# Two-batch score streaming, flat K transposes and a later norm and softmax in a decode-attention kernel

## The chip, the cores and the metric

The kernel runs on one core of one Trainium2 chip. The metric is device microseconds of one execution, and lower is better. Each run has a time, and a profile of one execution whose span is about 2 us shorter than its time. Some executions of a program are slower than the fastest of the same kernel by over 1.5%; they are called slow, and comparisons here use the others ("fast"). The *granted clock* is the share of full speed at which the profile shows TensorE running.

## The reference

Two independent problems, A and B, each a decode step of grouped-query attention with a window, are computed and joined at the end:

```python
# x (2,1,576)  wq (576,4096)  k_cache, v_cache (2,16,16384,128)  wo (4096,576), all bf16
q = (x @ wq).reshape(B, 1, 32, 128)              # 32 query heads, 16 key/value heads
k = repeat(k_cache[:, :, Sk-4096:], 2, axis=1)   # the last 4096 positions
v = repeat(v_cache[:, :, Sk-4096:], 2, axis=1)
p = softmax(einsum("bhqd,bhkd->bhqk", q, k) * 128**-0.5)
out = einsum("bhqk,bhkd->bhqd", p, v).reshape(B, 1, 4096) @ wo
# ... the same for B, then concatenated along the last axis
```

Each key/value head needs 2 MB of K and 2 MB of V (both batches), used once. With wq and wo the kernel reads 153.1 MB.

## The kernel before

A *slab* is one key/value head of one problem, both batches together: 32 slabs in all. Four slabs make a *group*, and the softmax runs once per group. Partitions hold (row, batch) pairs, so the kernel turns each K slab round before its score matmuls. VectorE does that with block transposes of fp32 words (each two bf16 values; 3592 ns for 128 x 2048 words in the profile of before). The kernel's patterns take a row in blocks of 32 words that hold both batches mixed, and the old transpose sorts the batches apart while it writes:

```python
# X: half a K slab, 128 x 2048 fp32 words; the write jumps between the batches' halves of a block
Xop[(t, jb)] = S.add("dve", lambda e: e.transpose(
    xt[:, n % NXT, :].bitcast(FP32).rearrange("p (c b r) -> p c r b", b=Bb, r=16),
    ring[:, r, jb * HW_:(jb + 1) * HW_].bitcast(FP32).rearrange("p (c r b) -> p c r b", b=Bb, r=16)), deps, ...)
# S: scores, one batch at a time, 8 matmuls of 512 columns for a half slab
for b in range(Bb):
    for p4 in range(4):
        o = 64 * b32 + 32 * b + par
        mv = bass.AP(b0.tensor, b0.offset, [list(b0.ap[0]), [128, 32], [2, 16]])
        last = e.matmul(st[:, 0:512], zq[:, p4, m, b, 16 - 16 * jb:144 - 16 * jb], mv, ...)
```

After the exps, P is transposed (pT), and four masked multiplications build pC, which has zeros where a V row belongs to the other batch. PV multiplies 64 tiles of V by 56 columns of pC. The *norm* divides by the softmax's sum. Instructions of an engine run in the order in which this loop adds them (in the slab shown further down, the transpose at 196.65 us starts only after the norm, for which VectorE had waited 3.75 us):

```python
for t in range(NSLAB + LAG):                 # LAG = 4
    i = t - LAG
    if t < NSLAB:
        for jb in range(2):
            make_X(t, jb)                    # VectorE
            make_S(t, jb)                    # TensorE
        # ... make_Z
        if t % 4 == 3:
            make_chain(t // 4)               # max, bias, exp, pT, pC, sum: all engines
    if i >= 0:
        make_PV(i)                           # TensorE
        make_norm(i)                         # VectorE: waits for PV(i)
        # ... projection
```

K and V slabs pass through a ring of eight slots. One queue issues the loads (q1 of the page, 153.10 MB), in the order of the program. A slot is loaded anew when its last reader (the second transpose for K, PV for V) is done. The *lag* is the number of slabs by which PV follows the K transposes in the loop.

Of the kernel before, what the change touches and what calls it, by code (L numbers as in the profile page):

```python
# [59 lines left out]
def build_kernel(nc, probs, out):  # L60
# [3 lines left out]
    LAG = 4  # L64
# [12 lines left out]
    SCALE = float(Dh) ** -0.5  # L77

# [14 lines left out]
    with es:  # L93
# [5 lines left out]
        zq = sb("zq", [128, 4, 4, 2, 144], BF16)  # L99
# [3 lines left out]
        qs = sb("qs", [128, NPROB, 4, Hq * Bb], BF16)  # L103
# [6 lines left out]
        pmask = sb("pmask", [128, 2], FP32)  # L110
        bmask = sb("bmask", [128, 4], FP32)
        hmask = sb("hmask", [128, 8], FP32)
        m1 = sb("m1", [128, 1], FP32)
        nM = sb("nM", [1, 16], FP32)
        nMrep = sb("nMrep", [1, 128], FP32)
        bias_sb = sb("bias_sb", [128, 1], FP32)
# [5 lines left out]
        pT = sb("pT", [128, 2, 512], BF16)  # L122
        PCW = 1024
        pC = sb("pC", [128, 2, PCW + 64], BF16)
# [6 lines left out]
        ST = [ps("st%d" % i) for i in range(2)]  # L131
        OT = [ps("ot%d" % i) for i in range(2)]
        PJ = [ps("pj%d" % i) for i in range(2)]
# [61 lines left out]
        p_zq = S.add("pool", lambda e: e.memset(zq[:].rearrange("d p m b w -> d (p m b w)").bitcast(FP32), 0.0), [], "zero_zq")  # L195
        p_zpc = S.add("pool", lambda e: e.memset(pC[:, :, PCW:PCW + 64], 0.0), [], "zero_pC")

        d_xs0 = S.add("dve", lambda e: e.memset(xtf[0:Bb, 0:NPROB * 4 * D].bitcast(FP32), 0.0), [], "zero_xs")

        def f_xs(e):  # L200
            last = None
            for h in range(2):
# [4 lines left out]
        d_pm = S.add("dve", lambda e: e.tensor_reduce(pmask[:, 0:2], ident_f[:].rearrange("p (i t) -> p t i", t=2), AX.X, ALU.add),  # L207
                     [p_ident_f], "pmask")
# [37 lines left out]
        for P in range(NPROB):  # L246
# [22 lines left out]
            def f_qs(e, bank, P=P):  # L269
# [6 lines left out]
                qs[:, P, :, :], bank[:, 0:256].rearrange("d (p w) -> d p w", p=4), ACTF.Copy), [op], "qsev%d" % P)  # L276
# [25 lines left out]

        def contiguous_wo(G):
            return G < NG - 1

# [51 lines left out]
        pC_op = {}  # L357
# [6 lines left out]
        def make_Z(t):  # L364
            P, g = t // Hkv, t % Hkv
            m = t % 4
            deps = [qs_ev[P], p_zq, d_bm]
            if t >= 4:
                deps.append(Sop[(t - 4, 1)])

            def f(e):
                last = None
                for p4 in range(4):
                    b0 = zq[:, p4, m, 0, 16 + 4 * m:16 + 4 * m + 1]
                    dst = bass.AP(b0.tensor, b0.offset, [list(b0.ap[0]), [32, 4], [144 + 2, Bb], [1, 2]])
                    src = qs[:, P, p4, 4 * g:4 * g + 4].rearrange("d (h b) -> d b h", b=Bb).unsqueeze(1).broadcast_to([128, 4, Bb, 2])
                    msk = bmask[:, 0:4].unsqueeze(2).unsqueeze(3).broadcast_to([128, 4, Bb, 2])
                    last = e.tensor_tensor(dst, src, msk, ALU.mult)  # L378
                return last
            Zop[t] = S.add("pool", f, deps, "Z%d" % t)  # L380

        def make_X(t, jb):
# [7 lines left out]
            else:  # L390
                deps.append(op_xT)
            Xop[(t, jb)] = S.add("dve", lambda e: e.transpose(  # L392
                xt[:, n % NXT, :].bitcast(FP32).rearrange("p (c b r) -> p c r b", b=Bb, r=16),
                ring[:, r, jb * HW_:(jb + 1) * HW_].bitcast(FP32).rearrange("p (c r b) -> p c r b", b=Bb, r=16)),
                deps, "X%d_%d" % (t, jb))
# [3 lines left out]
        def make_S(t, jb):  # L399
            G, m = t // 4, t % 4  # L400
            n = 2 * t + jb
            st = ST[G % 2]
            deps = [Xop[(t, jb)], Zop[t]]
            if m == 0 and jb == 0 and G >= 2:
                deps.append(exp_op[G - 2])

            def f(e):
                last = None
                for b in range(Bb):
                    for p4 in range(4):  # L410
                        b32, par = p4 // 2, p4 % 2
                        o = 64 * b32 + 32 * b + par
                        b0 = xt[:, n % NXT, o:o + 1]
                        mv = bass.AP(b0.tensor, b0.offset, [list(b0.ap[0]), [128, 32], [2, 16]])
                        first = m == 0 and jb == 0 and b == 0 and p4 == 0
                        last = e.matmul(st[:, 0:512], zq[:, p4, m, b, 16 - 16 * jb:144 - 16 * jb], mv,  # L416
                                        start=first, stop=True, skip_group_check=True)
                return last
            Sop[(t, jb)] = S.add("pe", f, deps, "S%d_%d" % (t, jb))

        APH = dict(a=8, p=8, h=2)

        def make_chain(G):
# [3 lines left out]
            mx = S.add("dve", lambda e: e.tensor_reduce(m1[:], st[:, :], AX.X, ALU.max), [Sop[(4 * G + 3, 1)]] + prev("Tm"), "max%d" % G)  # L427
            n1, b1, tm = tb_job(lambda e, bank: e.transpose(bank[0:1, 0:128], m1[:, 0:1], ident_f[:]), "Tm%d" % G, [mx, p_ident_f])  # L428
            chain[(G, "Tm")] = tm
            nm = S.add("dve", lambda e: e.tensor_reduce(nM[0:1, 0:16].rearrange("o (p h) -> o p h", p=8),  # L430
                                                        b1[0:1, 0:128].rearrange("o (a p h) -> o p h a", **APH),
                                                        AX.X, ALU.max, negate=True), [tm] + prev("nMrep"), "nM%d" % G)
            tb_consumer[n1] = nm
            chain[(G, "nMrep")] = S.add("dve", lambda e: e.tensor_scalar(  # L434
                nMrep[0:1, :].rearrange("o (a c) -> o a c", a=8), nM[0:1, 0:16].unsqueeze(1).broadcast_to([1, 8, 16]),
                SCALE, None, ALU.mult), [nm] + prev("bias"), "nMrep%d" % G)
            n2, b2, bi = tb_job(lambda e, bank: e.matmul(bank[:, 0:1], nMrep[0:1, 0:128], ones_f[0:1, 0:1], start=True, stop=True),  # L437
                                "bias%d" % G, [chain[(G, "nMrep")], p_ones_f])
            chain[(G, "bias")] = bi
            bc = S.add("act", lambda e: e.activation(bias_sb[:, 0:1], b2[:, 0:1], ACTF.Copy),  # L440
# [3 lines left out]
            for w in range(2):  # L444
                def f_exp(e, w=w):
                    if w == 0:
                        dst = pR[:, 0, :].rearrange("p (q r x) -> p q x r", r=16, x=2)
                    else:
                        b0 = pR[:, 1, 1:2]
                        dst = bass.AP(b0.tensor, b0.offset, [list(b0.ap[0]), [32, 16], [-1, 2], [2, 16]])  # L450
                    return e.activation(dst, st[:, :].rearrange("p (q x r) -> p q x r", x=2, r=16), ACTF.Exp,  # L451
                                        bias=bias_sb[:, 0:1], scale=SCALE, **({"accum_out": rsum[:, 0:1]} if w == 0 else {}))
                exs.append(S.add("act", f_exp, [bc] + prev("Ts") + prev("pT%d" % w), "exp%d_%d" % (G, w)))
            exp_op[G] = exs[1]
            n3, b3, ts = tb_job(lambda e, bank: e.transpose(bank[0:1, 0:128], rsum[:, 0:1], ident_f[:]), "Ts%d" % G, [exs[0], p_ident_f])  # L455
            chain[(G, "Ts")] = ts
            pts = []
            for w in range(2):
                chain[(G, "pT%d" % w)] = S.add("dve", lambda e, w=w: e.transpose(pT[:, w, :], pR[:, w, :]),  # L459
                                               [exs[w]] + prev("pC"), "pT%d_%d" % (G, w))  # L460
                pts.append(chain[(G, "pT%d" % w)])
            deps = pts + [d_pm, p_zpc]
            if G >= 2:
                deps.append(PVop[4 * (G - 2) + 3])

            def f_pc(e):
                last = None
                for b in range(Bb):
                    for w in range(2):
                        jp = b ^ w  # L470
                        src = pT[:, w, :].rearrange("k (q s b h) -> k s q b h", q=16, s=8, b=Bb)[:, :, :, b, :]
                        dst = pC[:, v, 0:PCW].rearrange("k (s q j b h) -> k s q j b h", s=8, q=16, j=2, b=Bb)[:, :, :, jp, b, :]
                        last = e.tensor_scalar(dst, src, pmask[:, b:b + 1], None, ALU.mult)  # L473
                return last
            chain[(G, "pC")] = S.add("dve", f_pc, deps, "pC%d" % G)
            pC_op[G] = chain[(G, "pC")]
            sm = S.add("dve", lambda e: e.tensor_reduce(ssum[0:1, 0:16].rearrange("o (p h) -> o p h", p=8),
                                                        b3[0:1, 0:128].rearrange("o (a p h) -> o p h a", **APH),
                                                        AX.X, ALU.add), [ts] + prev("rs"), "ssum%d" % G)
            tb_consumer[n3] = sm  # L480
            chain[(G, "rs")] = S.add("dve", lambda e: e.reciprocal(rs[0:1, 0:16], ssum[0:1, 0:16]), [sm] + prev("rsbm"), "rs%d" % G)  # L481
            n4, b4, rb = tb_job(lambda e, bank: e.matmul(bank[:, 0:16], ones_f[0:1, 0:128], rs[0:1, 0:16], start=True, stop=True),  # L482
# [8 lines left out]
        def make_PV(i):  # L491
# [9 lines left out]
            for j0, j1, dma in parts:  # L501
                def f(e, j0=j0, j1=j1):
                    last = None
                    for j in range(j0, j1):
                        jb, q, jp = j // 32, (j % 32) // 2, j % 2
                        col = ((jb * 4 + m) * 16 + q) * 8 + jp * 4
                        last = e.matmul(ot[:, 0:NS], ring[:, r, j * 128:(j + 1) * 128], pC[:, v, col:col + NS],  # L507
                                        start=(j == 0), stop=(j == KR - 1))
# [196 lines left out]
```

## Time and profile before

| | before |
|---|---|
| time, median (its range) | 468.87 us (467.79 to 469.25) |
| span of the profiled execution (which took 467.26 us) | 465.5 us |
| queue of the loads, share of 16 engines | 79.6% |
| VectorE / TensorE busy | 58% / 62% |
| mean granted TensorE clock | 0.795 |

These are lines of the kernel before's page: the TensorE clock, the DMA share (tenths) and the rate in 40 slices of the span, the queue of the loads, the chain of waits that ended last, and three groups of instructions (busy time, mean ns of one, idle time of the engine before them and what ended it).

```profile
PEclk9958977787687877886796785878868777788779
DMA  8999999999999946999379974499848994897000
GB/s 355 435 412 428 428 427 427 422 430 429 416 370 429 401 183 265 427 429 418 127 306 429 377 315 182 176 424 405 352 190 327 429 423 188 336 394 275 1 0 4
...
q1 hardware_dynamic: 11700, 153.10, 79.6%
...
DVE 49%; PE 40%; DMA 6%; issue 3%; ACT 1%; SPq 0%
...
L392 DVE STREAM_TRANSPOSE xt<-ring 128x2048 f32<-128x2048 f32 x64 | 225.0, 3592 | 21.2 <-DMA ring<-in_A_k_cache_dram 21.2
L416 PE MATMUL st<-xt,zq 128*128 128x512 bf16 x512 | 166.3, 483 | 108.2 <-DVE xt L392 107.6
...
L522 DVE TENSOR_TENSOR oTg<-ot,rsb 128x4 bf16<-128x4 f32 x32 | 5.2, 162 | 123.0 <-PE ot L507 123.0
```

The rate row starts at a plateau of about 427 GB/s and later has holes (183, 127, 176). At 427 GB/s the 153.1 MB would take 359 us. So the loads could be 100 us faster than the kernel, and the chain holds VectorE and TensorE, not DMA. No engine is full, because they take turns. The norm itself is 5.2 us of work, but VectorE stands idle for 123 us in front of it.

One ordinary slab, from the timeline of the kernel before (start us, duration us, engine, line, operation, and in brackets the idle time before and what ended it):

```profile
185.78 7.05 DVE L392 STREAM_TRANSPOSE xt<-ring 128x2048 f32<-128x2048 f32 x2
...
189.42 5.46 PE L416 MATMUL st<-xt,zq 128*128 128x512 bf16 x16 [3.76 <-DVE xt L392]
...
194.72 1.81 PE L507 MATMUL ot<-pC,ring 128*128 128x56 bf16 x64
...
196.57 0.16 DVE L522 TENSOR_TENSOR oTg<-ot,rsb 128x4 bf16<-128x4 f32 x1 [3.75 <-PE ot L507]
196.65 3.59 DVE L392 STREAM_TRANSPOSE xt<-ring 128x2048 f32<-128x2048 f32 x1
```

VectorE transposes for 7.05 us, then waits 3.75 us until TensorE has done the second half's scores and PV, does a norm of 0.16 us, and only then begins the next slab: 10.87 us from transpose to transpose (196.65 - 185.78). Once per group a softmax stands between as well, with no K transpose beside it: from the maximum at 217.7 us to the first PV at 224.4.

### The profile page before, as it was taken

Reading aid. Unit: us, or ns where it says so; the run is one execution under the profiler, and the core shown is the slowest. Engines: PE = TensorE matmul, PEld = TensorE weight load, DVE = VectorE, ACT = ScalarE, POOL = GpSimd, SP = SyncE. Lnnn points to the kernel's source line nnn. Section 1 sums busy time; section 2 is a strip of 40 time slices with the busy share of each in tenths; the row PEclk is TensorE's granted clock in tenths of the full one; section 3 lists DMA queues with packets and bytes.
Section 4 is the critical chain, followed back from the end, with each engine's and each line's share of the span. In section 5 each row is a group of like instructions: output and inputs, shape, how many; then the busy total and the mean of one; then the engine's idle time right before and its main releaser. Section 6 shows DMA issues by size and latency. Waiting matters only on the chain.

```text
span 465.5 us, 6840 instructions
## 1 busy us (share of the span) xinstructions
PE 287.1 (62%) x3124; PEld 156.4 (34%) x3124; DVE 269.3 (58%) x206; ACT 19.4 (4%) x50; POOL 30.2 (6%) x144
## 2 busy tenths in 40 slices
PE   1556535665866658656555656575586665865667
PEld 1552112331533334222433314232153323422155
DVE  3029966566666636665664662656666663666530
ACT  1000010001000010001000010000100001000010
POOL 5100100000000000000000000000000000000000
PEclk9958977787687877886796785878868777788779
DMA  8999999999999946999379974499848994897000
GB/s 355 435 412 428 428 427 427 422 430 429 416 370 429 401 183 265 427 429 418 127 306 429 377 315 182 176 424 405 352 190 327 429 423 188 336 394 275 1 0 4
DMA packets 11741, 153.54 MB, mean 330 GB/s; under 512 B 1208, under 2 KB 2240, under 8 KB 2368
## 3 DMA queue, kind: packets, MB, share of 16 engines
q1 hardware_dynamic: 11700, 153.10, 79.6%
q8 instruction: 24, 0.39, 0.3%
q14 instruction: 5, 0.04, 0.0%
q10 hardware_dynamic: 12, 0.01, 0.0%
HBM read 153.10 MB, written 0.00 MB: 329 GB/s over the span
## 4 chain that ended last, share of the span: by engine, by line
DVE 49%; PE 40%; DMA 6%; issue 3%; ACT 1%; SPq 0%
DVE xt L392 40%; PE st L416 22%; PE ot L507 14%; DMA ring<-in_A_k_cache_dram 6%; DVE pT L459 2%; DVE pC L473 2%; PE pj L571 1%; DVE m L427 1%; DVE oTg L522 1%; PE tb L482 1%; ACT pR L451 1%; PE tb L437 1%; PE tb L551 1%; PE pj L539 1%; DVE nM L430 0%
## 5 line engine op out<-in xcount | busy, mean ns | idle before, releaser
L392 DVE STREAM_TRANSPOSE xt<-ring 128x2048 f32<-128x2048 f32 x64 | 225.0, 3592 | 21.2 <-DMA ring<-in_A_k_cache_dram 21.2
L416 PE MATMUL st<-xt,zq 128*128 128x512 bf16 x512 | 166.3, 483 | 108.2 <-DVE xt L392 107.6
L416 PEld LDWEIGHTS st<-xt,zq 128*128 128x128 bf16 x512 | 53.0, 114 | 212.1 <-DVE xt L392 138.0
L522 DVE TENSOR_TENSOR oTg<-ot,rsb 128x4 bf16<-128x4 f32 x32 | 5.2, 162 | 123.0 <-PE ot L507 123.0
L507 PEld LDWEIGHTS ot<-pC,ring 128*128 128x128 bf16 x2048 | 66.2, 102 | 6.7 <-issue 1.6
L507 PE MATMUL ot<-pC,ring 128*128 128x56 bf16 x2048 | 68.0, 196 | 0.0
L378 POOL TENSOR_TENSOR zq<-qs,bmask 128x16 bf16<-128x16 bf16 x128 | 23.5, 216 | 355.6 <-PE st L416 341.7
L571 PE MATMUL pj<-wob,oP 128*2 128x288 bf16 x112 | 24.1, 396 | 4.9 <-DVE oP L563 4.9
L459 DVE STREAM_TRANSPOSE pT<-pR 128x512 bf16<-128x512 bf16 x16 | 11.4, 712 | 12.6 <-ACT pR L451 12.6
L482 PE MATMUL tb<-rs,ones_f 1*128 1x16 f32 x16 | 4.8, 379 | 21.5 <-DVE rs L481 21.5
L254 PE MATMUL tb<-xU,ring 128*128 128x56 bf16 x288 | 12.5, 219 | 8.0 <-DMA ring<-in_B_wq_dram 5.8
L571 PEld LDWEIGHTS pj<-wob,oP 128*2 128x2 bf16 x112 | 11.8, 110 | 14.6 <-DVE oP L563 5.6
L427 DVE TENSOR_REDUCE m<-st 128x1 f32<-128x512 f32 x8 | 5.5, 691 | 19.3 <-PE st L416 19.3
L440 ACT ACTIVATE bias_sb<-tb 128x1 f32<-128x1 f32 x8 | 1.4, 171 | 364.1 <-PE tb L437 364.1
L254 PEld LDWEIGHTS tb<-xU,ring 128*128 128x128 bf16 x288 | 12.3, 119 | 8.2 <-DMA ring<-in_B_wq_dram 5.9
L451 ACT ACTIVATE pR<-st,bias_sb 128x512 bf16<-128x512 f32 x16 | 12.7, 818 | 0.3
L482 PEld LDWEIGHTS tb<-rs,ones_f 1*128 1x128 f32 x16 | 4.0, 305 | 23.3 <-DVE rs L481 23.3
L473 DVE TENSOR_SCALAR pC<-pT,pmask 128x256 bf16<-128x256 bf16 x32 | 8.4, 335 | 0.3
L236 PE MATMUL tb<-ident_b,xt 2*128 2x2 bf16 x36 | 2.3, 194 | 9.8 <-DVE xt L204 9.8
L455 PE MATMUL tb<-ident_f,rsum 128*1 128x128 f32 x8 | 2.5, 308 | 9.3 <-ACT pR L451 9.3
L437 PE MATMUL tb<-ones_f,nMrep 1*128 1x1 f32 x16 | 3.0, 256 | 4.9 <-DVE nMrep L434 4.9
L428 PE MATMUL tb<-ident_f,m 128*1 128x128 f32 x8 | 2.2, 270 | 6.3 <-DVE m L427 6.3
(42 smaller groups left out, 46.3 us busy)
## 6 DMA issues: line engine op xcount, KB each, us to landing
ring<-in_A_k_cache_dram SPq DMA_DIRECT2D x16, 2048.0 KB, 20.7
ring<-in_A_v_cache_dram SPq DMA_DIRECT2D x16, 2048.0 KB, 12.7
ring<-in_B_k_cache_dram SPq DMA_DIRECT2D x16, 2048.0 KB, 9.4
ring<-in_B_v_cache_dram SPq DMA_DIRECT2D x15, 2048.0 KB, 9.9
ring<-in_A_wq_dram SPq DMA_DIRECT2D x1, 4608.0 KB, 13.5
ring<-in_B_wq_dram SPq DMA_DIRECT2D x1, 4608.0 KB, 25.4
wob<-in_A_wo_dram SPq DMA_DIRECT2D x4, 1152.0 KB, 15.5
wob<-in_B_wo_dram SPq DMA_DIRECT2D x4, 1152.0 KB, 10.4
```

What stands on the lines that cost most here:

```text
L254: last = e.matmul(bank[:, c * 64:c * 64 + NS], wqv[P][:, u, cb * 128:(cb + 1) * 128], xU[:, P, u, 0:NS], start=(u == 0), stop=(u == NU - 1))
L378: last = e.tensor_tensor(dst, src, msk, ALU.mult)
L392: Xop[(t, jb)] = S.add("dve", lambda e: e.transpose(xt[:, n % NXT, :].bitcast(FP32).rearrange("p (c b r) -> p c r b", b=Bb, r=16), ring[:, ...
L416: last = e.matmul(st[:, 0:512], zq[:, p4, m, b, 16 - 16 * jb:144 - 16 * jb], mv, start=first, stop=True, skip_group_check=True)
L427: mx = S.add("dve", lambda e: e.tensor_reduce(m1[:], st[:, :], AX.X, ALU.max), [Sop[(4 * G + 3, 1)]] + prev("Tm"), "max%d" % G)
L451: return e.activation(dst, st[:, :].rearrange("p (q x r) -> p q x r", x=2, r=16), ACTF.Exp, bias=bias_sb[:, 0:1], scale=SCALE, **({"accum_ ...
L459: chain[(G, "pT%d" % w)] = S.add("dve", lambda e, w=w: e.transpose(pT[:, w, :], pR[:, w, :]), [exs[w]] + prev("pC"), "pT%d_%d" % (G, w))
L473: last = e.tensor_scalar(dst, src, pmask[:, b:b + 1], None, ALU.mult)
L482: n4, b4, rb = tb_job(lambda e, bank: e.matmul(bank[:, 0:16], ones_f[0:1, 0:128], rs[0:1, 0:16], start=True, stop=True), "rsbm%d" % G, [ch ...
L507: last = e.matmul(ot[:, 0:NS], ring[:, r, j * 128:(j + 1) * 128], pC[:, v, col:col + NS], start=(j == 0), stop=(j == KR - 1))
L522: norm_op[i] = S.add("dve", lambda e: e.tensor_tensor(oTg[:, v, 2 * m:2 * m + 2, :], OT[i % 2][:, 0:4].rearrange("d (b h) -> d h b", h=2), ...
L571: last = e.matmul(PJ[half][0:Bb, 0:NH], oP[:, v, j, :], wob[:, v, j, half * NH:(half + 1) * NH], start=(proj_start(G) and j == 0), stop=Tr ...
```

## The change

The intent has four parts. (a) The K transpose writes flat. (b) The *masked path*: score matmuls stream both batches' columns as they lie, into two banks per group; columns of the foreign batch get a bias of -1e30 in the exp and so become zeros, and transposed P feeds PV directly, without pC and its multiplications (so here the bias is the mask; "the old masked pC path" below means before's). (c) The norm comes after the next slab's first transpose, and the softmax is spread over the next group's first slab. (d) The lag goes from 4 to 5. The core of the diff, with cuts:

```diff
-    LAG = 4
+    LAG = 5
+    OFF = -1.0e30
...
             Xop[(t, jb)] = S.add("dve", lambda e: e.transpose(
-                xt[:, n % NXT, :].bitcast(FP32).rearrange("p (c b r) -> p c r b", b=Bb, r=16),
-                ring[:, r, jb * HW_:(jb + 1) * HW_].bitcast(FP32).rearrange("p (c r b) -> p c r b", b=Bb, r=16)),
-                deps, "X%d_%d" % (t, jb))
+                xt[:, n % NXT, :].bitcast(FP32), ring[:, r, jb * HW_:(jb + 1) * HW_].bitcast(FP32)), deps, "X%d_%d" % (t, jb))
...
-                for b in range(Bb):
+                for jl in range(2):
                     for p4 in range(4):
-                        o = 64 * b32 + 32 * b + par
+                        o = 2048 * jl + 64 * b32 + par
-                        mv = bass.AP(b0.tensor, b0.offset, [list(b0.ap[0]), [128, 32], [2, 16]])
+                        mv = bass.AP(b0.tensor, b0.offset, [list(b0.ap[0]), [128, 16], [2, 32]])
...
+            for jb in range(2):
+                def f_exp(e, jb=jb):
+                    for t in range(2):          # columns of batch t: foreign rows have the bias OFF
+                        last = e.activation(pR[:, jb, :].rearrange("p (x t) -> p t x", t=2)[:, t, :],
+                                            st[jb][:, :].rearrange("p (x t) -> p t x", t=2)[:, t, :], ACTF.Exp,
+                                            bias=bias_sb[:, t:t + 1], scale=SCALE, accum_out=...)
...
-                        last = e.matmul(ot[:, 0:NS], ring[:, r, j * 128:(j + 1) * 128], pC[:, v, col:col + NS],
+                        last = e.matmul(ot[:, 0:NS], ring[:, r, j * 128:(j + 1) * 128], pT[:, v, col:col + NS],
...
-        for t in range(NSLAB + LAG):
+        for t in range(NSLAB + LAG + 1):
             i = t - LAG
+            # X(t,0) S(t,0) | max, bias, exp of group t//4-1 when t%4 == 0 | norm(i-1) |
+            # X(t,1) S(t,1) | pT, sum of that group | PV(i) | projection
```

## The prediction

> **What bounds it now.** Not the transfers. The page's 40 slices show about 427 GB/s at first, then holes (183, 127, 176); 153.1 MB at 427 would take 359 us, the span is 465.5. The queue's own waits: 208 us for the K transpose, 133 for PV; consumers free the eight slots too late. The chain of waits alternates VectorE's K transposes (40%), scores (22%) and PV (14%). In the timeline an ordinary slab is two transposes of 3.52 us, scores (1.90 us, 3.4 at half clock), PV 1.67-1.81, and a norm of 0.16 that in-order VectorE awaits 3.7-5.9 us before the next transpose: 10.8-12.6 us. Once per four slabs the softmax (217.7 to 227.5 us) runs with no K transpose beside it. A group takes about 54 us; its transfers need 4 x 9.8 + 2.8 = 42.
>
> **What changes.**
> 1. Order. Norm and softmax move half a slab or more later: under the next transpose TensorE does scores and PV, under the second exp runs. With the old transpose time, an ordinary slab becomes scores 2.6 + PV 2.1 (means over both clocks) + 0.3 + 3.5 = 8.5 us; a group's first about 16 (the transposes of max and sum queue behind scores), its second 10.7: 44 us a group.
> 2. Flat K transpose. It writes consecutive fp32 words, not words 64 bytes apart. The 512-element pT takes 712 ns; [...]2048 would be about 2.3 us, not 3.59. [...]If so, 64 x 1.25 = 80 us of VectorE go, and a group needs 37 us. Chance 70%.
> 3. pC goes: 32 x 335 ns, 1 us a group.
> 4. Added: a second maximum per group (+0.7 us), doubled small max and bias work (1 us), four half-size exps with four accumulator reads for two (+0.7 us, hidden). TensorE's work is unchanged: 512 score matmuls of 512 columns, 2048 of PV. Strided PSUM reads may cost a little.
> 5. Lag 5 for 4: one more slab at the end, hidden behind V loads.
>
> **How much is on the path.** Nearly all of 1-3, until transfers bind. With the fast transpose a group (37 us) is under its loads (42): bound by transfers. The first 116 us move 48.8 MB at 419 GB/s, the other 104.3 MB at 428 take 244: last byte near 361 us. Then short PV, norm, projection, copy, output: 4 us as at before's end; 1.8 from span to device time. About 368. With the old transpose: first scores near 32, 44 a group, a tail of 20: about 392. Weighted: **371 us, 8 in 10 from 364 to 396**. Faster by over 2%: 0.98; within 2%: 0.01; slower: 0.01.
>
> **What would show it.** DMA at 9 in every slice until the end; the queue's waits for consumers down; the transpose's waits for K loads up; mean transpose 2.3 us (3.5 is the miss); no pC lines; norm's wait for PV (123 us) below 40; VectorE busy about 190 us; mean clock about 0.8.
>
> **What would make it wrong.** The transpose stays at 3.5 us (390 or more); stride-2 PSUM reads double maxima and exps; score matmuls read xt or write PSUM slower; half clock for most of the time, so that scores plus PV take 10 us a slab; group-boundary waits that hold the ring; wo loads, held in order behind a projection, that open holes.

The 2.3 us stands as a forecast only ("If so" refers to it). The sum: 64 x 1.25 = 80 us of VectorE, 37 us a group, branches of 368 and 392 us, and 371 put between them.

## The result, and the profile after

| | before | after |
|---|---|---|
| time, median (range), 4 runs each | 468.87 (467.79 to 469.25) | 371.17 us (370.97 to 372.71) |
| span | 465.5 | 369.0 us |
| queue of the loads | 79.6% | 98.0% |
| VectorE busy | 269.3 | 185.9 us |
| mean granted clock | 0.795 | 0.857 |

The ratio is 0.793, 95% interval 0.790 to 0.795. A ratio here is always the mean time of one kernel's fast runs over that of the other's in the same rounds, so not quite the ratio of the medians. The lines of the changed kernel's page that answer to those of before:

```profile
PEclk9978999898589888998588888999578886996898
DMA  8999999999999999999999999999999999999992
GB/s 320 448 414 426 426 425 433 428 426 426 429 424 424 426 423 435 424 428 426 423 431 424 426 426 427 430 425 428 420 430 428 427 423 426 428 424 420 424 418 121
...
q1 hardware_dynamic: 11700, 153.10, 98.0%
...
DMA 87%; DVE 10%; PE 2%; SPq 1%; issue 0%
...
L392 DVE STREAM_TRANSPOSE xt<-ring 128x2048 f32<-128x2048 f32 x64 | 146.0, 2292 | 100.7 <-DMA ring<-in_A_k_cache_dram 56.5
L413 PE MATMUL st_0<-xt,zq 128*128 128x512 bf16 x256 | 78.1, 457 | 53.4 <-DVE oTg L532 28.5
...
L532 DVE TENSOR_TENSOR oTg<-ot,rsb 128x4 bf16<-128x4 f32 x32 | 4.3, 134 | 16.6 <-PE ot L517 16.5
```

The holes are gone and the chain is loads. VectorE now waits 100.7 us for K to land, where before it was 21.2. The issuing queue's waits for the transposes fell from 208 to 146 us and those for PV from 133 to 47. The norm's wait is 16.6 us. An ordinary slab in the changed kernel's timeline:

```profile
243.56 2.28 DVE L392 STREAM_TRANSPOSE xt<-ring 128x2048 f32<-128x2048 f32 x1
...
245.90 1.92 PE L413 MATMUL st_1<-xt,zq 128*128 128x512 bf16 x8 [0.34 <-DVE xt L392]
...
247.63 2.31 DVE L392 STREAM_TRANSPOSE xt<-ring 128x2048 f32<-128x2048 f32 x1 [1.79 <-DMA ring<-in_B_k_cache_dram]
247.66 1.81 PE L517 MATMUL ot<-pT,ring 128*128 128x56 bf16 x64
...
249.87 0.12 DVE L532 TENSOR_TENSOR oTg<-ot,rsb 128x4 bf16<-128x4 f32 x1
249.91 2.29 DVE L392 STREAM_TRANSPOSE xt<-ring 128x2048 f32<-128x2048 f32 x1
```

PV runs under the next slab's first transpose, and the norm finds it done. The last PV starts at 364.2 us, so 4.8 us of the span lie behind the last wait for a load.

So the total came out as predicted. That it did so to 0.2 us of the median is luck: 371 was put between two branches, 368 with a fast transpose and 392 without (weighted 70 to 30 they make 375), and the branch that came true said 368. Nor does the total show that the reasons were right: several changes went in together, and a floor hides which of them were needed. The experiments take them apart.

### The profile page after: what moved, and what is told of

Read it like the earlier page. It is cut to its first block, busy times and chain, and to the rows that moved or that the text cites. A ratio compares the mean times of both kernels' runs of the same rounds, so it can differ in the third digit from the quotient of the medians.

```text
span 369.0 us, 6842 instructions
## 1 busy us (share of the span) xinstructions
PE 251.1 (68%) x3148; PEld 146.9 (40%) x3148; DVE 185.9 (50%) x213; ACT 23.0 (6%) x90; POOL 15.3 (4%) x49
## 4 chain that ended last, share of the span: by engine, by line
DMA 87%; DVE 10%; PE 2%; SPq 1%; issue 0%
DMA ring<-in_B_k_cache_dram 41%; DMA ring<-in_A_k_cache_dram 40%; DVE xt L392 9%; DMA ring<-in_B_v_cache_dram 6%; PE st_0 L413 1%; PE ot L517 1%; SPq L348 0%; SPq L174 0%; DVE mx L422 0%; DVE oTg L532 0%; DVE out_sb L594 0%; PE pj L549 0%
## 5 line engine op out<-in xcount | busy, mean ns | idle before, releaser
L392 DVE STREAM_TRANSPOSE xt<-ring 128x2048 f32<-128x2048 f32 x64 | 146.0, 2292 | 100.7 <-DMA ring<-in_A_k_cache_dram 56.5
L413 PE MATMUL st_0<-xt,zq 128*128 128x512 bf16 x256 | 78.1, 457 | 53.4 <-DVE oTg L532 28.5
L413 PE MATMUL st_1<-xt,zq 128*128 128x512 bf16 x256 | 77.5, 454 | 30.6 <-DVE xt L392 30.6
L517 PEld LDWEIGHTS ot<-pT,ring 128*128 128x128 bf16 x2048 | 63.9, 100 | 13.2 <-DMA ring<-in_B_v_cache_dram 5.0
L517 PE MATMUL ot<-pT,ring 128*128 128x56 bf16 x2048 | 64.6, 193 | 3.8 <-DMA ring<-in_B_v_cache_dram 3.8
L413 PEld LDWEIGHTS st_0<-xt,zq 128*128 128x128 bf16 x256 | 25.1, 108 | 91.8 <-DVE oTg L532 30.7
L413 PEld LDWEIGHTS st_1<-xt,zq 128*128 128x128 bf16 x256 | 26.4, 110 | 73.0 <-DVE xt L392 36.8
L379 POOL TENSOR_TENSOR zq<-qs,bmask 128x64 bf16<-128x64 bf16 x32 | 9.3, 294 | 282.9 <-PE st_1 L413 267.8
L532 DVE TENSOR_TENSOR oTg<-ot,rsb 128x4 bf16<-128x4 f32 x32 | 4.3, 134 | 16.6 <-PE ot L517 16.5
L452 PE MATMUL tb<-ones_f,nMrep 1*128 1x1 f32 x32 | 6.0, 288 | 6.0 <-DVE nMrep L446 6.0
L452 PEld LDWEIGHTS tb<-ones_f,nMrep 1*128 1x128 f32 x32 | 5.3, 234 | 9.2 <-DVE nMrep L446 9.2
L463 ACT ACTIVATE pR<-st_0,bias_sb 128x256 bf16<-128x256 f32 x16 | 8.2, 542 | 0.3
L463 ACT ACTIVATE pR<-st_1,bias_sb 128x256 bf16<-128x256 f32 x16 | 8.2, 548 | 0.0
L584 PE MATMUL pj<-wob,oP 128*2 128x288 bf16 x112 | 8.0, 285 | 0.0
```

What stands on the lines that cost most here:

```text
L379: return e.tensor_tensor(dst, src, msk, ALU.mult)
L392: Xop[(t, jb)] = S.add("dve", lambda e: e.transpose(xt[:, n % NXT, :].bitcast(FP32), ring[:, r, jb * HW_:(jb + 1) * HW_].bitcast(FP32)), d ...
L413: last = e.matmul(st[:, 0:512], zq[:, p4, m, 16 - 16 * jl:144 - 16 * jl], mv, start=(m == 0 and jl == 0 and p4 == 0), stop=True, skip_grou ...
L452: last = e.matmul(bank[:, t:t + 1], nMrep[0:1, t, :], ones_f[0:1, 0:1], start=True, stop=True)
L463: last = e.activation(pR[:, jb, :].rearrange("p (x t) -> p t x", t=2)[:, t, :], st[jb][:, :].rearrange("p (x t) -> p t x", t=2)[:, t, :], ...
L517: last = e.matmul(ot[:, 0:NS], ring[:, r, j * 128:(j + 1) * 128], pT[:, v, col:col + NS], start=(j == 0), stop=(j == KR - 1))
```

## The experiments

My theory, as of the prediction: the order (c, d) and the flat transpose (a) would each take about 75 us alone, and the loads cap their sum; the masked path (b) is neutral. The lag (d) was only changed together with the order, never on its own. Rival 1: the transpose is everything. Rival 2: dropping pC and the masks (b) carries a real part. The three parts make eight combinations, of which six had to be built. Unless said otherwise a kernel had four runs in three timed rounds and a profile; "before" in the same rounds had medians of 464.7, 468.3 and 467.0 us.

One bench below permutes K on purpose and still passed the comparison, probably because these inputs give nearly flat softmaxes (the scales in the reference make scores of about 0.001). A pass thus says little about which column went where. That the variants compute the right thing rests on their layouts.

### new_order_only: the order and the lag, on the old data path

```diff
-    LAG = 4
+    LAG = 5
-        for t in range(NSLAB + LAG):  ...      # the loop of before
+        for t in range(NSLAB + LAG + 1):  ...  # the loop of the changed kernel
+        # make_chain cut in three, make_proj in two, as the changed kernel has them; contents as before
```

> The kernel before with the changed kernel's order of instructions and lag of 5, but the old scattered K transpose and the old pC path. My theory (order and flat transpose each would take about 75 us alone, and the loads cap their sum): about 392 us, 380 to 405, a mean transpose of 3.5 us, VectorE busy about 270 us, holes left in the DMA row, DMA share about 93%. Rival 1 (the transpose is all, order alone does little): above 440. Rival 2 (removing pC and the masks carries a real part): above 405, since pC is still in the chain.

Measured: 371.39 us (370.99 to 373.7), ratio 0.798. This is the whole gain, with the old scattered transpose and with pC. The forecast of 392 was wrong. Its page shows how:

```profile
q1 hardware_dynamic: 11700, 153.10, 97.8%
...
PE 43%; DVE 37%; DMA 17%; issue 2%; ACT 0%; SPq 0%
...
L392 DVE STREAM_TRANSPOSE xt<-ring 128x2048 f32<-128x2048 f32 x64 | 227.0, 3607 | 21.4 <-DMA ring<-in_A_k_cache_dram 21.1
```

The queue is full as in the changed kernel, but the chain here is four fifths compute and only 17% loads: both end at about the same time. Rival 1 falls. Rival 2 falls as far as time at full loads goes.

### flat_only: the flat transpose alone, old order, old path

```diff
-   xt[...].bitcast(FP32).rearrange("p (c b r) -> p c r b", b=Bb, r=16), ring[...].rearrange("p (c r b) -> p c r b", ...)
+   xt[:, n % NXT, :].bitcast(FP32), ring[:, r, jb * HW_:(jb + 1) * HW_].bitcast(FP32)
-   o = 64 * b32 + 32 * b + par
+   o = 64 * b32 + 2 * b + par
-   mv = bass.AP(b0.tensor, b0.offset, [list(b0.ap[0]), [128, 32], [2, 16]])
+   mv = bass.AP(b0.tensor, b0.offset, [list(b0.ap[0]), [128, 32], [4, 16]])
```

> The kernel before with only the K transpose written flat; the score matmuls pick each batch's columns with a step of 8 bytes. My theory: the transpose drops to 2.3 us and nearly all of 64 x 1.25 = 80 us leaves, less where scores at half clock (3.4 us) now outlast a transpose: about 395 us, 385 to 410, norm still waiting over 100 us for PV. Rival 1 (the transpose is all): at or under 380. If the step of 8 bytes costs TensorE, scores take over 2 us at full clock and the time is above 410.

Measured: 470.91 us (469.76 to 471.36), ratio 1.011: nothing gained, though the transposes did get 81 us shorter. Groups on its page, and a line of its timeline:

```profile
L414 PE MATMUL st<-xt,zq 128*128 128x512 bf16 x512 | 225.7, 608 | 56.8 <-DVE xt L392 56.5
L392 DVE STREAM_TRANSPOSE xt<-ring 128x2048 f32<-128x2048 f32 x64 | 144.0, 2285 | 26.4 <-DMA ring<-in_A_k_cache_dram 23.3
...
L520 DVE TENSOR_TENSOR oTg<-ot,rsb 128x4 bf16<-128x4 f32 x32 | 5.2, 161 | 180.0 <-PE ot L505 180.0
...
L425 DVE TENSOR_REDUCE m<-st 128x1 f32<-128x512 f32 x8 | 5.5, 690 | 42.8 <-PE st L414 42.8
```

```profile
212.50 7.06 PE L414 MATMUL st<-xt,zq 128*128 128x512 bf16 x16 [2.47 <-DVE xt L392]
```

The expectation's last sentence names what happened. After a flat transpose, one batch's columns lie 8 bytes apart. The starts of successive weight loads show the pace of these matmuls. From the same kernel's timeline of weight loads, two at half clock and two at full clock, and then the windows that hold them (the number before the last two, 0.50 and 0.99, is the granted clock):

```profile
215.07 0.12 PEld L414 LDWEIGHTS st<-xt,zq 128*128 128x128 bf16 x1 [0.31 <-issue]
215.50 0.12 PEld L414 LDWEIGHTS st<-xt,zq 128*128 128x128 bf16 x1 [0.31 <-issue]
...
217.66 0.11 PEld L414 LDWEIGHTS st<-xt,zq 128*128 128x128 bf16 x1 [0.32 <-issue]
218.09 0.11 PEld L414 LDWEIGHTS st<-xt,zq 128*128 128x128 bf16 x1 [0.32 <-issue]
```

```profile
215.00:217.00 2.00, 2.00 (x6) 0.61 (x5) 0.00 (x0) 0.00 (x0) 0.00 (x0) 0.50 1.04 369
217.00:219.50 2.50, 2.50 (x6) 0.45 (x4) 0.00 (x0) 0.00 (x0) 0.00 (x0) 0.99 0.97 360
```

They start 0.43 us apart in both: a full clock no longer helps. Sixteen matmuls took 7.06 us. With a step of 4 bytes sixteen took 3.73 us at full clock in new_order_only. Scores went from 166.3 us in before to 225.7 us busy. VectorE's wait for PV grew from 123.0 to 180.0 us and its wait for scores before the maximum from 19.3 to 42.8: together 80.5 us, all that the transposes gave.

### new_order_flat: new order and flat transpose, still with pC

The edits of the two above together.

> The kernel before with new order, lag 5 and flat transpose, still with the old masked pC path. My theory: bound by its loads like the changed kernel, 369 to 375 us, DMA share 97 to 98%, no holes. Rival 2 (the path without pC is needed): above 378.

Measured: 393.76 us (393.62 to 396.39), ratio 0.847: 22 us *worse* than the order alone. TensorE is 83% busy (scores 227.6 us) and its chain share is 76%. My theory (369 to 375) was wrong: I had not given the slow read a place in it. The number is rival 2's (above 378), but in a new form: with flat transposes the path without pC is needed, not for pC's sake but because it lets TensorE read all columns at a step of 4 bytes (at full clock 0.23 us a matmul in new_order_only, against 0.43 at 8 bytes in flat_only).

### masked_path_only: streaming both batches, no pC, with old order and old transpose

```diff
 # on the changed kernel: loop and lag of before, the scattered transpose, and
-   st[jb][:, :].rearrange("p (x t) -> p t x", t=2), AX.X, ALU.max)
+   st[jb][:, :].rearrange("p (q t r) -> p t q r", t=2, r=16), AX.XY, ALU.max)
 # (exps read the same view; maxima and exps thus still see each batch's columns)
```

> The changed kernel's data path (both batches in two score banks, bias of -1e30 for foreign columns, no pC, exps by parity) with the old order, lag 4 and the old scattered transpose. My theory: pC's 1 us a group is about paid back by the second maximum and the doubled small steps: 460 to 472 us, 466 likely. Rival 2 (removing pC and the masks carries a real part of the gain): under 455.

Measured: 471.42 us (469.9 to 471.53), ratio 1.011. By itself (b) gains nothing, as I expected.

### scattered_in_new and old_order_in_new: the two remaining combinations

scattered_in_new is the changed kernel with the edit of masked_path_only but its own order. old_order_in_new is the changed kernel with the loop and the lag of before.

> The changed kernel with the old scattered K transpose; maxima and exps read the scores in the order that this leaves, so the result is right. My recorded estimate for this was 392 us. The first four runs speak against it: new order alone, with the scattered transpose, took 371.4. New theory (the order alone brings every group under its 42 us of loads; the flat transpose only adds slack): 370 to 376 us, transpose 3.5 us, DMA share 97 to 98%. Rival (the masked path with its second maximum is just too long without the flat transpose, which is why the two came together): 380 to 392.

> The changed kernel with the old order and lag 4: flat transpose and both batches streamed, scores read with a step of 4 bytes. Flat transpose alone in the old path gained nothing, because scores with a step of 8 bytes started every 432 ns at any clock. If that is the whole reason, here the transpose's gain shows: per slab 2.4 us less VectorE in series, less what scores at half clock eat: 392 to 420 us, 405 likely. If flat transposes are worth nothing in the old order for another reason: above 455.

Measured: scattered_in_new 374.21 us (373.41 to 376.83), ratio 0.801, the queue full in every slice but the last ones. old_order_in_new 399.32 us by its three fast runs (395.55 to 400.64; a fourth, slow, took 401.8), ratio 0.852. Both came as the new theory said. All eight combinations, medians in us ("before" itself varies by 4 us):

| | scattered transpose | flat transpose |
|---|---|---|
| old order, old path (pC) | 468.9 (before) | 470.9 |
| old order, masked path | 471.4 | 399.3 |
| new order, old path (pC) | 371.4 | 393.8 |
| new order, masked path | 374.2 | 371.2 (after) |

In the old order, (a) and (b) gain nothing each and about 69 us together (468.3 to 399.3 in their own rounds). In the new order everything that is not spoiled by the 8-byte read stands at 371 to 374.

### norm_late_only and softmax_late_only: which part of the order

```diff
 # norm_late_only: loop of before, LAG = 4, but
+   make_X(t, 0); make_S(t, 0); make_norm(i - 1); make_X(t, 1); make_S(t, 1); ...; make_PV(i)
 # softmax_late_only: LAG = 5, chain parts placed as in the changed kernel, but
+   make_PV(i); make_norm(i)
```

> The kernel before with one part of the order: a slab's norm (and the spread and projection after it) comes behind the next slab's first K transpose; softmax stays where it was, lag 4. If the norm's wait is most of the gain: an ordinary slab falls from about 11 to 8 us, a group from 54 to 43: about 395 us, 385 to 410. If it is the softmax: above 440.

> The kernel before with the other part of the order: max, bias, exp, pT and pC spread over the next group's first slab, lag 5; each norm still directly behind its PV. If both parts count, about 10 us less 2 in each of 8 groups goes: about 405 us, 395 to 420. If the norm's wait is nearly all: above 440.

Measured: norm_late_only 386.46 us (385.92 to 389.23), ratio 0.828; softmax_late_only 440.67 us (439.41 to 442.14), ratio 0.943. The later norm gives most, 82 us off its baseline of 468.3; the later softmax 28 us. Their sum, 110 us, is more than the 93 us that both together gain (464.7 to 371.4 in their own rounds). The loads' floor is not the main reason: with half of V taken away (next section) both together still gain only 98 us (467.0 to 369.2). So the two parts overlap; where they do is not shown. From the page of norm_late_only:

```profile
L416 PE MATMUL st<-xt,zq 128*128 128x512 bf16 x512 | 138.4, 418 | 72.0 <-DVE xt L392 67.9
...
L531 DVE TENSOR_TENSOR oTg<-ot,rsb 128x4 bf16<-128x4 f32 x32 | 5.2, 161 | 28.4 <-PE ot L516 27.0
```

With the late norm VectorE's wait for PV is 27.0 us (123.0 before). TensorE's wait for transposes in front of scores fell from 107.6 to 67.9 us; with it went a mean granted clock of 0.862 (0.795 before), and the scores' busy time fell from 166.3 to 138.4 us. The softmax forecast of 405 was too good; what it saves is under half of what I took.

### half_v_after, half_v_new_order, half_v_scattered: what is there under the floor

```diff
+   half = SW // 2 if kind == "V" else SW
-   e.dma_start(ring[:, r, :], src)
+   e.dma_start(ring[:, r, 0:half], src[:, :, 0:half])
```

The same edit on three kernels. Results are wrong (relative error 0.67).

> The changed kernel, but each V load except the last brings only its first half; PV runs over old data in the other half, so the result is wrong on purpose. 33 MB less to load: the loads would end near 285 us. Theory (the loads bind the changed kernel and compute has slack): time falls to about 330 us (37 us a group), 315 to 345, with holes in the DMA row. Rival (compute binds as much as the loads): 360 or more.

> The kernel before with the new order alone, V loads halved in the same way, wrong on purpose. Its chain of waits was compute for four fifths at full loads, so it should be at its edge: 355 to 370 us, clearly over the changed kernel with halved loads. That difference is what flat transpose and masked path are worth once the loads do not bind. Rival (they are worth nothing at all): within 2% of the changed kernel with halved loads.

> The changed kernel with the scattered transpose and halved V loads, wrong on purpose. If the flat transpose is the worth of the data path: about the same as the new order alone with halved loads, or a few us more (second maximum): 355 to 375. If dropping pC and the masks is worth something by itself: 10 us or more under it.

Measured: half_v_after 301.92 and 304.51 us in its two fast runs, mean 303.2 (two slow ones took 308.72 and 310.53). half_v_new_order has a median of 369.15 us (five runs, 367.51 to 373.54, the longest one slow; mean of the fast ones 369.2). half_v_scattered took 373.55 (373.44 to 374.23). The span and the rates of half_v_after, then of half_v_new_order:

```profile
span 302.5 us, 6842 instructions
...
GB/s 313 439 416 421 425 431 425 426 428 425 425 412 424 429 422 426 429 420 427 426 427 419 425 433 411 429 422 424 421 427 425 425 424 423 421 363 386 422 86 6
```

```profile
span 370.9 us, 6834 instructions
...
GB/s 319 445 417 429 422 425 425 432 392 422 422 351 228 228 410 413 386 193 303 441 422 180 266 427 426 368 213 258 355 353 313 219 327 428 291 0 136 429 133 3
```

Taking 33 MB away changed new order alone and the scattered version by less than 1%: both are bound by compute at the time they also have with full loads. The changed kernel fell by 68 us (371.2 to 303.2), below the 315 to 345 forecast and without the holes that were forecast: its loads hardly paused until about 285 us. So flat transpose and masked path together are worth about 66 us (369.2 - 303.2) with these halved loads, but only where loads do not bind. The chain of half_v_after is already three quarters compute (PE 50%, DVE 24%, DMA 23%), so still smaller loads may bring little more; that was not tried. Since half_v_scattered is no faster than half_v_new_order, dropping pC without the flat transpose is again worth nothing.

The times between a group's maximum and the next (VectorE's timeline, first to last, over seven groups): half_v_new_order 41.0 us (62.3 to 349.0), half_v_after 32.2 us (53.4 to 278.6). Full loads of a group, four times two slabs at 4.9 us and wo at 2.8 (2048 and 1152 KB at 427 GB/s), are 42 us; with half V they are 32.2. These means hold short intervals at both ends: counted in the same way, the changed kernel with full loads has 40.8 us (53.3 to 339.0). Over the five middle intervals it has 42.5 (90.4 to 303.1), and half_v_new_order 41.9 (100.3 to 309.6). So the order alone lands within 1 us of the full loads, by luck of the sizes.

### patterns: what the steps cost

A bench inside the changed kernel, one profile and one run (414.09 us, state unknown), wrong on purpose:

```diff
+   XP = [1, 2, 4, 8, 16, "pair", 1, 16]    # step between successive fp32 words written, by 2*(t%4)+jb
+   e.transpose(xpat(xt..., 2*(t%4)+jb), rpat(ring..., 2*(t%4)+jb))
+   # scores of slots 1 to 4 read 512 columns with a step of 1, 2, 4, 8 bf16; slots 5, 6 the two old forms
```

> A bench inside the changed kernel, wrong on purpose: the eight K transposes of a group write with steps of 4, 8, 16, 32 and 64 bytes, in pairs 16 bytes apart, and twice as controls; the score matmuls read with steps of 2, 4, 8 and 16 bytes beside the two old forms. [...]transposes 2.3 us at 4 and 8 bytes and in pairs, about 3.5 at 16, 32 and 64; score matmuls 216 ns apart at full clock at 2 and 4 bytes, slower at 8 and 16, since 4 bytes passed and 8 bytes took 432 ns. If instead any pattern but one run costs VectorE: 3.5 at all steps above 4 bytes.

The transposes of one group in the bench's timeline of VectorE. In order: step of 8 bytes; of 16; of 32 and of 64 together; pairs 16 bytes apart and flat together; of 64 and, for the next group, flat together.

```profile
151.83 2.29 DVE L410 STREAM_TRANSPOSE xt<-ring 128x2048 f32<-128x2048 f32 x1
...
158.35 3.75 DVE L410 STREAM_TRANSPOSE xt<-ring 128x2048 f32<-128x2048 f32 x1
...
164.89 7.29 DVE L410 STREAM_TRANSPOSE xt<-ring 128x2048 f32<-128x2048 f32 x2
...
175.39 4.49 DVE L410 STREAM_TRANSPOSE xt<-ring 128x2048 f32<-128x2048 f32 x2
...
189.56 5.72 DVE L410 STREAM_TRANSPOSE xt<-ring 128x2048 f32<-128x2048 f32 x2
```

At 8 bytes and in pairs the transpose costs what a flat one does (2.29 us; 4.49 for a pair-wise and a flat one). At 16, 32 and 64 bytes it costs 3.5 to 3.75. So it is not "any pattern" that costs: the slow ones write every word 16 bytes or more from the one before, and in the pairs every second word lies next to the one before. The old kernel's 64-byte step paid that in all 64 transposes (3592 ns on average, 2292 flat).

For TensorE, again by the starts of weight loads: two with a step of 8 bytes, at half clock, and two with a step of 16; then the window of the latter, with a clock of 1.00.

```profile
170.07 0.13 PEld L439 LDWEIGHTS st<-xt,zq 128*128 128x128 bf16 x1 [0.33 <-issue]
170.53 0.12 PEld L439 LDWEIGHTS st<-xt,zq 128*128 128x128 bf16 x1 [0.33 <-issue]
...
178.96 0.12 PEld L439 LDWEIGHTS st<-xt,zq 128*128 128x128 bf16 x1 [0.78 <-issue]
179.86 0.12 PEld L439 LDWEIGHTS st<-xt,zq 128*128 128x128 bf16 x1 [0.78 <-issue]
```

```profile
177.20:180.00 2.80, 2.80 (x4) 0.42 (x4) 2.68 (x2) 0.00 (x0) 0.00 (x0) 1.00 0.96 407
```

16 bytes take 0.90 us even at full clock. For 8 bytes flat_only gave 0.43 us at full clock. With steps of 2 and of 4 bytes the bench's trace has seven matmuls in 1.67 and in 1.74 us at full clock (one record of each eight is missing); the weight loads of these start 0.216 and 0.226 us apart. So TensorE slows already at 8 bytes and again at 16: at full clock the time of 512 columns about doubles, from 4 bytes on, with each doubling of the step (0.226, 0.43, 0.90 us), while from 2 to 4 bytes it hardly moves (0.216 to 0.226). VectorE's transposes take 2.29 us at 8 bytes as they do flat, and between 16 and 64 bytes they stay at 3.5 to 3.75. What the limit is in either engine is not shown; the runs show the times by step.

## Why the prediction was right, and where it was wrong

- **Bound by loads after the change: right.** Queue share 98.0%, chain 87% loads, and in half_v_after fewer loads made it faster at once. "Last byte near 361 us" was 3 us early, as the last PV starts at 364.2.
- **Flat transpose about 2.3 us, 70%: right.** 2292 ns, and VectorE lost 79 us (225.0 to 146.0) where 80 was forecast. The runs show 1.03 ns for each further element between before's pT and the flat transpose (2292 - 712 ns over 2048 - 512), an estimate across two types (bf16 and fp32). The bench shows what the time goes with: with a step of 8 bytes the transpose took 2.29 us, with every word 16 bytes or more from the one before 3.5 to 3.75. The cause is not shown.
- **"How much is on the path: nearly all of 1-3, until transfers bind": wrong for the transpose.** In flat_only not one of its 81 us showed; with the masked path beside it 69 us showed in the old order (old_order_in_new), and 3 in the new one (374.2 to 371.2), which stands at the loads without it. In the old path a flat layout makes TensorE read with 8-byte steps and moves the time from VectorE (81 us less in transposes) to the scores (166.3 to 225.7 us busy) and to VectorE's waits for TensorE (80.5 us more). The prediction took "TensorE's work is unchanged" for the whole change, which is true there (scores 166.3 to 155.6 us, both banks), but missed that this is what (b) is for.
- **"With the old transpose ... about 392": wrong.** scattered_in_new took 374.2, new order alone 371.4. The mis-sized term is the group with old transposes, 44 us, measured 41.0 in half_v_new_order: at its loads (41.9 against 42.5 over the middle intervals), not above. The parts of one group there (182 to 223 us), from VectorE's timeline: first slab 14.3 us (16 forecast), second 9.8 (10.7), the other two 9.5 and 7.3 (8.5 each). So most of the excess lay in the group's first two slabs; why they were forecast too long stays open, as the prediction does not split them up. The ordinary slab, where I had added scores and PV with means over both clocks (4.7 us), was right on average (8.4 in this group); where the clock is full it is 7.4 us (new_order_only, 204.25 to 211.61 us, clock 1.00 from 206.1 to 209.9), as scores of 1.9 and PV of 1.8 us pass almost wholly under a transpose of 3.6.
- **A group with the flat transpose, 37 us: too high.** half_v_after shows 32.2 us, which is its loads, so compute needs no more than that.
- **pC, masks, second maximum about even: right.** masked_path_only was 1.1% slower, scattered_in_new 3 us slower than new order alone (their ratios, 0.801 and 0.798, do not differ clearly).
- **Strided reads of scores "may cost a little": for the maxima they did not.** Maxima over every other word took 657 and 676 ns, over all words 691 before. The exps have no counterpart of the same size to compare with.
- **Norm's wait below 40 us, VectorE about 190 us, clock about 0.8:** 16.6, 185.9 and 0.857. The clock was a little above the forecast. The windows show it at half, at full, or a mix of both (0.50, 0.99 and 1.00 above; 0.73 in flat_only from 212.5 to 215). In norm_late_only TensorE waited less for transposes (67.9 us for 107.6) and the mean clock was higher (0.862 for 0.795); what sets the clock is not shown.

The time was met because the fast transpose, on which most weight lay, does lead to the loads' floor; but the order alone leads there too. The 24 us that the estimate put between the two branches (368 and 392) do not exist: scattered_in_new is 3 us slower. No run points to a version faster than the changed kernel. Both it and new order alone stand at the loads; it has slack under them and the other has none.

## What to carry to other kernels

When an engine works in order, look for the short instruction that waits for another engine in front of long independent work; moving the norm behind one transpose was worth 82 us and touched no arithmetic. When a change meets a floor, its parts cannot be judged by the total: lower the floor in an experiment (here half of V) to see which parts make slack and which do nothing. A layout that makes the writer faster can make the reader slower, so look at the steps on both sides before crediting the gain; here the transposes gave 81 us and the scores' step of 8 bytes took it all back.
